# Attention and two feed-forward parts on one core: the identity for the row maxima read from PSUM instead of SBUF

## The chip, the cores and the metric

The kernel runs on one core of a Trainium2 chip. Its engines work beside one another and wait for each other through semaphores: TensorE (PE, with PEld for its weight loads), VectorE (DVE), ScalarE (ACT), GpSimd (POOL) and SyncE (SP), which issues most transfers. The metric is device time in microseconds (us), from several runs, and less is better.

## The reference, cut to what matters

First comes attention over 4 batches of 8 heads, with 576 positions of 64 features, in float32. It is causal by blocks of 64 positions. After it come two feed-forward parts, which the change doesn't touch.

```python
scores = scale * np.matmul(q, k.transpose(0, 1, 3, 2))
mask = block_i >= block_j                      # blocks of 64 positions
scores = np.where(mask, scores, -1000000000.0)
scores = scores - np.max(scores, axis=-1, keepdims=True)
attn = np.exp(scores)
attn = attn / (np.sum(attn, axis=-1, keepdims=True) + 1e-09)
return np.matmul(attn, v).astype(np.float32)
...
x = _moe_ref(x=x, **moe_kwargs)                # first feed-forward part
return _moe2_ref(x=x, **moe2_kwargs)           # second one, with a normalisation
```

## The kernel before, in words

The attention is a loop over 34 units: 32 heads ("h"), and two units ("z") for the first 64 positions of the batches, which are handled apart. A head's scores lie transposed in a PSUM tile `s` of 128 partitions by 1536 columns (three banks): partitions are keys, columns are queries. The list `SEG` says which key tile has which columns. Key tile 4 has only 64 keys, so in its 64 columns (960 to 1023 of the tile) only partitions 0 to 63 are of use; before the change its product is formed on all 128 partitions, with zeros for the missing keys.

A head goes through these steps, and each step of the loop holds one step of several heads.

- `em_A` forms the first products into `s` (five matrix products). It is sent a step ahead.
- `chain` finds the largest score of each query. VectorE reduces the five column ranges with a transposing maximum (L374), fills three places of `part` that belong to masked blocks with three memsets (L377), reduces again (L380), ScalarE brings four groups of 32 partitions together (`r<-r`, three instructions), VectorE reduces once more (L406) and writes the row of maxima on the diagonals of 32x32 blocks: the product of the maxima, broadcast, and a 32x32 identity, broadcast (L408). The result goes into 32 partitions of the right operand of the next products, `QK`.
- `em_B` adds the second products into `s` (five matrix products). They hold the low parts of queries and keys, the mask and, through the rows that L408 wrote, minus the maximum. So they wait for L408. Then ScalarE takes the exponential (`e<-s`).
- `em_PV` multiplies with the values (`p<-e,V`), and `norm` divides by the sums: VectorE by L455, L456 and L457, GpSimd by L458.

TensorE gets its work in the order em_A of head i+1, em_B of head i, em_PV of head i-1. The order on every engine is written out by hand. GpSimd meanwhile subtracts rounded parts from raw ones for later heads (L43, by `split_q` and `split_k`), and VectorE, ScalarE and GpSimd convert the weights of the first feed-forward part in between (L121, L125 on VectorE), at places that the table `PIECES` gives. The identity `eye` is a 128x128 tile in SBUF that a transfer brings at the start. `s` comes from a pool of two buffers, anew for each unit.

```python
tt(out=v3(dst)[:, x:x + 16],                     # L408
   in0=m[:, x:x + 16].unsqueeze(2).to_broadcast([32, 16, 32]),
   in1=eye[0:32, 0:32].unsqueeze(1).to_broadcast([32, 16, 32]), op=ALU.mult)
```

Of the kernel before, what the change touches and what calls it, by code (L numbers as in the profile page):

```python
# [25 lines left out]
GORD = (0, 3, 4, 2, 1)  # L26
# a head's score columns: (key tile, first query, queries, column)
SEG = [(0, 64, 512, 0), (1, 128, 448, 512), (4, 512, 64, 960), (2, 256, 320, 1024), (3, 384, 192, 1344)]
# [3 lines left out]
def attention_moe_kernel(ctx, tc, raw_d, dup_d, raw0_d, dup0_d, v_d, v0_d, msk_d, mz_d, vec_d, eye_d, wk_d, wv_d, wr_d, wc1_d, wc2_d, out_d):  # L32
# [43 lines left out]

    # A weight comes as the bits of a float64: sign, 11 bits of exponent, 52 of fraction. It
    # is loaded three bytes off, so that word 0 of its pair holds the exponent's low 4 bits
    # and 28 of the fraction, and byte 4 the sign and the exponent's high 7 bits, e. A
    # float32's sign and high 4 bits of exponent are those of e - 56, nothing below 56.  # L80
    CE = float(56 * 2 ** 27)

    def load_split(src, dst):
        """512 columns of a weight: as a float32, its rounded part and the rest; in steps, of one or two instructions."""
        st = {}
# [52 lines left out]
    def pieces(w, dst, k, n):  # L138
        """Rows 128k.. of w, n columns."""
        return [load_split(w[:, f:f + 512], lambda i, f=f: dst(i)[:, k, f:f + 512]) for f in range(0, n, 512)]  # L140

    class Convert:
        """Weight pieces on their way, one step per call."""

# [29 lines left out]

# [1 line left out]
    sp = opened(es_a, "as", 2, side=R)  # L176
# [16 lines left out]
    units.insert(IZ + 1, ("z", (1, 2, 3)))  # L193
    # The first 64 positions of several batches make one unit, whose operands lie where the
    # last weights come in later.
    wv0, wv1, wk0 = [w.rearrange("p k n -> p (k n)") for w in (*wv, wk[0])]
# [3 lines left out]
    LZ, QZ = wv1[:, 0:1536], wv1[:, 1536:3072]  # L200
    VZ = XT[B - 2][:, :, 65:577].rearrange("p b (k d) -> p b k d", d=128)
    N = len(units)
    idx = {u: i for i, u in enumerate(units)}
# [9 lines left out]
    def kz(a):  # L213
        """Batch a's operands of the first products, and its raw ones."""
        return KZ[:, 1024 * a - 1024:1024 * a], XT[B - 1][:, a - 1, 65:577]
# [17 lines left out]
    def make(u, who):  # L233
        """The first units' operands out of what load_raw brings, in parts, each by one of the engines."""
        t, n = u
        kl, qb = ops_B(u)
        raw = T.pop(("raw", u))
        w = 576 if t == "h" else 512
        if t == "z":
            kq = wk0[:, 0:1024]  # L240
        else:
            if n == 0:
                T["kq", 0] = lp.tile([128, 2, 1088], F32R, name="kq")
            kq = T["kq", 0][:, n]
        T["kq", u] = kq
        L, H, Q = slice(0, w), slice(w, w + 512), slice(w - 512, w)
        lo, up = slice(0, 64), slice(64, 128)

        def copy(x, out, in_):
            if x == "a":  # L250
                act(out, in_)
            else:
                (nc.vector if x == "d" else nc.gpsimd).tensor_copy(out=out, in_=in_)

        def less(x, out, in0, in1):
            sub(nc.vector if x == "d" else nc.gpsimd, out, in0, in1)

        return [
            lambda: copy(who[0], kq[lo, L], raw[lo, L]),
            lambda: copy(who[1], kq[up, H], raw[up, Q]),  # L260
            lambda: copy(who[2], kq[up, L], raw[lo, L]),
            lambda: copy(who[3], kq[lo, H], raw[up, Q]),
            lambda: less(who[4], kq[up, H], raw[up, Q], kq[up, H]),
            lambda: copy(who[5], qb[lo, Q], raw[up, Q]),
            lambda: less(who[6], kl[lo, L], raw[lo, L], kq[lo, L]),
        ]

    def joint_z(a, steps):
        """Batch a's part of what the joint unit needs."""
        kq, raw = kz(a)  # L270
# [24 lines left out]
    def tail_z(u):  # L295
        """Division by the sums, an instruction each."""
        n = len(u[1])
# [38 lines left out]
    def mm(out, lhsT, rhs, start, stop=True, **kw):  # L336
        nc.tensor.matmul(out=out, lhsT=lhsT, rhs=rhs, start=start, stop=stop, **kw)  # L337

    def em_A(u):
        s = ps.tile([128, 1536], F32, name="s")  # L340
        T["s", u] = s
        if u[0] == "h":
            kq = T["kq", u]
            for (j, q0, w, o) in SEG:
                mm(s[:, o:o + w], kq[:, 128 * j:128 * j + 128], kq[:, 512 + q0:512 + q0 + w], o % 512 == 0, skip_group_check=True)
        else:
            for x, b in enumerate(u[1]):
                kq = T["kq", u] if b == 0 else kz(b)[0]
                for o in range(0, 512, 128):
                    mm(s[:, 512 * x + o:512 * x + o + 128], kq[:, o:o + 128], kq[:, 512 + o:640 + o], o == 0, skip_group_check=True)  # L350

    def ops_B(u):
        """The second products' operands."""
        return (LZ, QZ) if u[0] == "z" else (KL[idx[u] % NB], QB[idx[u] % NB])

    def v3(ap):
        return ap.rearrange("p (b i) -> p b i", i=32)

    def chain(u):
        """From the first products to the row of maxima, in parts."""  # L360
        s = T["s", u]
# [4 lines left out]
        if u[0] == "h":  # L366
# [3 lines left out]
            def first():  # L370
                for (j, q0, w, o) in sorted(SEG, key=lambda x: x[0] == 0):
                    kp = 128 if j < 4 else 64
                    b0 = (q0 - 64) // 32
                    red(out=pt[0:kp, b0:b0 + w // 32, j], in_=v3(s[0:kp, o:o + w]), axis=AX.X, op=ALU.max, apply_transpose=True)  # L374
                for j in (1, 2, 3):
                    b0 = (128 * j - 64) // 32
                    ms(pt[64:128, b0:b0 + 2, j], -3.0e38)  # L377

# [13 lines left out]
        def mid():  # L392
# [14 lines left out]
        ] + [  # L407
            lambda x=x: tt(out=v3(dst)[:, x:x + 16], in0=m[:, x:x + 16].unsqueeze(2).to_broadcast([32, 16, 32]), in1=eye[0:32, 0:32].unsqueeze(1).to_broadcast([32, 16, 32]), op=ALU.mult)  # L408
            for x in range(0, nb, 16)
        ]  # L410

    def em_B(u):
# [4 lines left out]
        if u[0] == "h":  # L417
            for (j, q0, w, o) in SEG:
                mm(s[:, o:o + w], kl[:, 128 * j:128 * j + 128], qb[:, q0:q0 + w], False, skip_group_check=True)
            act(e, s, AF.Exp, scale=0.125)  # L420
        else:
            w = 512 * len(u[1])
            for o in range(0, w, 128):
                mm(s[:, o:o + 128], kl[:, o:o + 128], qb[:, o:o + 128], False, skip_group_check=True)
            act(e[:, 0:w], s[:, 0:w], AF.Exp, scale=0.125)

    def em_PV(u, x=0):
# [13 lines left out]
    def norm(u):  # L441
        """Division by the sums; parts for the step after em_PV(u)."""
        n = u[1]
# [16 lines left out]

# [1 line left out]
    def segs(g):  # L462
# [7 lines left out]
    def prep(g, kk, c, X):  # L470
        """A mixture of 128 features (by column c + kk of vec), split into X; in steps."""
        m = tmp.tile([128, GT], F32, name="mix")
# [71 lines left out]

# [1 line left out]
    groups = [(512 * i, min(512, NTOK - 512 * i)) for i in range(-(-NTOK // 512))]  # L546
# [74 lines left out]

    # When the first weights' steps come, by the attention's iterations: from the first one
    # on, a letter each. l: load; 1, 2: the exponent's two parts; x, y: the bits' two
    # instructions, X, Y: the same late in the iteration, B: x and Y; h: rounded; w, v, V: the
    # rest, by GpSimd or VectorE.
    PIECES = [
        (1, "l.12Bhw"), (4, "l12B.hw"), (6, "l12x.y.hw"), (9, "l1.2XyhV"), (17, "l12Bhv"),
        (21, "l12Bhw"), (22, "l12.x.yhw"), (27, "l12Bhw"), (29, "l12BhV"),
    ]
    # The joint unit's: its masks; per batch the load, three instructions and two engines;  # L630
    # its tail's ten instructions. Halves are late in an iteration.
    MASKS_Z = 2
    READY_Z = (4, 5.5, 10.5, 8.5, nc.gpsimd, nc.vector), (6, 11.5, 9.5, 13, nc.vector, nc.vector), (7, 12, 12.5, 12, nc.gpsimd, nc.gpsimd)
    TAIL_Z = 18, 18, 18.5, 20, 23, 22.5, 21, 23.9, 22.9, 21.9
    with tc.manual_schedule():
        # ---- attention, one step per unit
        plan = {}
# [11 lines left out]
        ms(eps, 1e-6)  # L649
        act(rsd[:, 0:1], eps, AF.Exp)  # loads the function's table  # L650
        ms(ce, -CE)
        for i in (0, 1):
            ms(part[i], -3.0e38)
        masks_z(0, 1)
        masks(1)
# [112 lines left out]

        # ---- the first feed-forward part
        es_h, es_r = ExitStack(), ExitStack()  # L770
# [55 lines left out]

        # ---- the second feed-forward part; its start runs beside the end of the first's
        es_f = ctx.enter_context(ExitStack())
# [50 lines left out]

        # the next weights' steps at three places of a step, by the group  # L880
        first = (0, 0, 0), (0, 0, 1), (0, 0, 0), (0, 1, 1), (1, 1, 2)
# [3 lines left out]
        def norms(x):  # L885
            """The next groups' part of the normalisation."""
            if x + 1 < len(GORD):
# [94 lines left out]
```

## Time and profile before

| what | value |
|---|---|
| median of 3 runs | 889.67 us |
| lowest and highest run | 888.71 and 891.22 us |
| span of the profiled execution, first to last instruction | 889.8 us |
| busy in the span: PE, DVE, ACT, POOL | 836.4, 558.3, 403.3, 266.8 us |
| mean granted TensorE clock | 0.983 of full speed |

The profile is of one execution. No other time of that execution is given than its span, which is 0.1 us above the median of the runs, so the span is used as its time. The attention takes about the first 220 us of it, the rest is the two feed-forward parts.

### The profile page before, as it was taken

How to read it: one execution, taken by the hardware profiler on the slowest of the kernel's cores; microseconds unless marked ns; L12 is line 12 of the kernel's file. 1: busy time of each engine (PE TensorE's matmuls, PEld its weight loads, DVE VectorE, ACT ScalarE, POOL GpSimd, SP SyncE). 2: the span in 40 equal slices, each digit the busy share in tenths (PEclk: the TensorE clock that was granted, in tenths of full speed). 3: DMA queues.
4: the chain of work that ended last, by engine and by line, in shares of the span. 5: the costliest groups of instructions: out<-in, count | busy, mean ns of one | idle time of the engine just before them, and what ended most of it. 6: DMA issues, size and time to landing. Idle time of an engine off the chain costs nothing. (4 is left out here: it accounts for less than half of the span.)

```text
span 889.8 us, 10495 instructions
## 1 busy us (share of the span) xinstructions
PE 836.4 (94%) x3824; PEld 678.8 (76%) x3824; DVE 558.3 (63%) x977; ACT 403.3 (45%) x689; POOL 266.8 (30%) x217
## 2 busy tenths in 40 slices
PE   4878888798978999999999999999999999999998
PEld 3555564565856898898898888888888888888886
DVE  6899899989899524414438756546555554536433
ACT  5867686778766543543554343312232222313110
POOL 6768567765577301101102311101101010101100
PEclk9989898989999999999999999999999999999999
DMA  9994366552332012001234311201111110201023
GB/s 241 286 311 154 123 207 217 161 161 63 121 127 72 12 60 71 23 14 36 72 142 127 122 40 56 72 24 48 47 49 48 48 48 24 71 1 48 1 95 118
DMA packets 40068, 83.65 MB, mean 94 GB/s; under 512 B 3472, under 2 KB 17936, under 8 KB 40016
## 3 DMA queue, kind: packets, MB, share of 16 engines
q1 hardware_dynamic: 34544, 60.61, 20.8%
q0 software_dynamic: 5040, 20.01, 7.5%
q10 hardware_dynamic: 432, 2.36, 0.8%
q8 instruction: 30, 0.49, 0.2%
q14 instruction: 22, 0.18, 0.1%
HBM read 71.17 MB, written 11.80 MB: 93 GB/s over the span
## 5 line engine op out<-in xcount | busy, mean ns | idle before, releaser
L337 PE MATMUL ph<-xn,c 128*128 128x512 f32 (+1 forms) x960 | 205.6, 369 | 0.0
L337 PE MATMUL po<-c,h 128*128 128x512 f32 x864 | 204.3, 391 | 0.4 <-DVE acc L618 0.4
L337 PEld LDWEIGHTS ph<-xn,c 128*128 128x128 f32 x960 | 167.9, 188 | 31.8
L337 PEld LDWEIGHTS po<-c,h 128*128 128x128 f32 x864 | 161.5, 188 | 35.6 <-DVE acc L618 1.2
L40 ACT ACTIVATE h<-ph 128x512 fp32r<-128x512 f32 (+1 forms) x80 | 42.9, 553 | 220.1 <-PE ph L337 220.1
L43 POOL TENSOR_TENSOR c<-a,c 128x512 fp32r<-128x512 f32 x32 | 42.1, 1317 | 310.3 <-ACT c L40 240.0
L604 DVE SCALAR_TENSOR_TENSOR h<-ph,h 128x512 fp32r<-128x512 f32 (+1 forms) x80 | 49.8, 636 | 129.5 <-ACT h L40 129.5
L618 DVE TENSOR_TENSOR acc<-po,acc 128x512 f32<-128x512 f32 x144 | 97.8, 688 | 45.7 <-PE po L337 43.8
L337 PE MATMUL p<-e,V 128*128 128x512 f32 (+4 forms) x320 | 112.6, 483 | 0.0
L337 PE MATMUL s<-x,wk 128*128 128x384 f32 x576 | 103.5, 339 | 1.3 <-DVE x L43 1.2
L337 PEld LDWEIGHTS s<-x,wk 128*128 128x128 f32 x576 | 101.3, 188 | 3.2 <-DVE x L43 1.4
L40 ACT ACTIVATE a<-raw,ce 128x512 f32<-128x512 int8 x93 | 66.9, 754 | 77.1 <-DVE a L125 58.5
L337 PE MATMUL p<-wv,k 128*128 128x512 f32 x432 | 99.4, 390 | 0.0
L337 PEld LDWEIGHTS p<-e,V 128*128 128x128 f32 (+1 forms) x320 | 56.7, 202 | 49.6 <-issue 42.4
L337 PEld LDWEIGHTS p<-wv,k 128*128 128x128 f32 x432 | 80.9, 188 | 16.5
L43 POOL TENSOR_TENSOR x<-mix,x 128x384 fp32r<-128x384 f32 x36 | 41.6, 1172 | 156.2 <-ACT x L40 152.9
L43 DVE TENSOR_TENSOR k<-a,k 128x768 fp32r<-128x768 f32 x24 | 23.6, 983 | 81.6 <-ACT a L40 81.5
L374 DVE TRANSPOSE_TENSOR_REDUCE part<-s 128x14 f32<-128x448 f32 (+4 forms) x160 | 64.5, 460 | 5.5 <-PE s L337 4.9
L125 DVE SCALAR_TENSOR_TENSOR a<-raw,a 128x512 int32<-128x512 int32 x52 | 58.8, 1130 | 3.8
L40 ACT ACTIVATE e<-s 128x1536 f32<-128x1536 f32 (+1 forms) x34 | 48.3, 1421 | 28.4 <-PE s L337 28.2
L337 PE MATMUL s<-QK 128*128 128x512 f32 (+4 forms) x160 | 35.2, 353 | 26.7 <-DVE QK L408 25.9
L337 PE MATMUL s<-wr,x 128*128 128x512 f32 x216 | 53.4, 407 | 6.3 <-ACT x L40 5.3
(105 smaller groups left out, 894.3 us busy)
## 6 DMA issues: line engine op xcount, KB each, us to landing
kq<-in_dup_dram POOLq DMA_DIRECT2D x15, 1088.0 KB, 5.7
raw<-in_raw_dram SPq DMA_DIRECT2D x32, 288.0 KB, 4.9
raw<-in_w_ch_dram SPq DMA_DIRECT2D x16, 511.6 KB, 3.7
raw<-in_w_ch_dram SPq DMA_DIRECT2D x32, 255.6 KB, 3.1
V<-in_v_dram SPq DMA_DIRECT2D x16, 320.0 KB, 4.6
x_scr<-r SPq DMA_DIRECT2D x18, 256.0 KB, 2.0
acc<-x_scr SPq DMA_DIRECT2D x18, 256.0 KB, 4.7
out_dram<-acc SPq DMA_DIRECT2D x18, 256.0 KB, 2.0
```

The costliest lines, as they stand in the source:

```text
L40: nc.scalar.activation(out=out, in_=in_, func=func, **kw)
L43: eng.tensor_tensor(out=out, in0=in0, in1=in1.bitcast(F32), op=ALU.subtract)
L125: stt(out=st["a2"].bitcast(I32), in0=w3, scalar=5, in1=st["a1"].bitcast(I32), op0=ALU.logical_shift_right, op1=ALU.bitwise_or)
L337: nc.tensor.matmul(out=out, lhsT=lhsT, rhs=rhs, start=start, stop=stop, **kw)
L374: red(out=pt[0:kp, b0:b0 + w // 32, j], in_=v3(s[0:kp, o:o + w]), axis=AX.X, op=ALU.max, apply_transpose=True)
L604: stt(out=h1[1][:, m, 0:n], in0=p[:, 0:n], scalar=0.0, in1=h1[0][:, m, 0:n].bitcast(F32), op0=ALU.max, op1=ALU.subtract)
L618: tt(out=acc[i], in0=p, in1=acc[i], op=ALU.add)
```

## The change: what it does

The two tiles for scores are taken from the pool once (`SC`) and used in turn. In each, a 32x32 identity is kept in partitions 64 to 95 of columns 960 to 991, where no useful score lies. So that nothing overwrites it, the products of key tile 4 are cut to 64 columns of weights and write partitions 0 to 63 alone, in `em_A` and in `em_B` (`seg`). ScalarE writes the identity (`put_eye`) at the start, after VectorE has filled the place with zeros, and once more after the joint unit of three batches, which uses the whole tile. L408 of a head reads its second operand from there; L408 of the two "z" units reads `eye` as before. The three memsets at L377 become one whose pattern visits the same places. The other lines of the diff only drop comments.

```diff
+    SC = [ps.tile([128, 1536], F32, name="s") for _ in range(2)]
...
+    def seg(x, j):
+
+        k = 128 if j < 4 else 64
+        return x[:, 128 * j:128 * j + k], slice(0, k)
+
+    def put_eye(s):
+        act(s[64:96, 960:992], eye[64:96, 64:96])
+
     def em_A(u):
-        s = ps.tile([128, 1536], F32, name="s")
+        s = SC[idx[u] % 2]
...
             for (j, q0, w, o) in SEG:
-                mm(s[:, o:o + w], kq[:, 128 * j:128 * j + 128], kq[:, 512 + q0:512 + q0 + w], o % 512 == 0, skip_group_check=True)
+                k, P = seg(kq, j)
+                mm(s[P, o:o + w], k, kq[:, 512 + q0:512 + q0 + w], o % 512 == 0, skip_group_check=True)
...
+    def strided(x, *steps):
+
+        return bass.AP(x.tensor, x.offset, [list(x.ap[0])] + [list(a) for a in steps])
...
-                for j in (1, 2, 3):
-                    b0 = (128 * j - 64) // 32
-                    ms(pt[64:128, b0:b0 + 2, j], -3.0e38)
+
+                ms(strided(pt[64:128, 2:4, 1], [21, 3], [5, 2]), -3.0e38)
...
-            lambda x=x: tt(out=v3(dst)[:, x:x + 16], in0=m[:, x:x + 16].unsqueeze(2).to_broadcast([32, 16, 32]), in1=eye[0:32, 0:32].unsqueeze(1).to_broadcast([32, 16, 32]), op=ALU.mult)
+            lambda x=x: tt(out=v3(dst)[:, x:x + 16], in0=m[:, x:x + 16].unsqueeze(2).to_broadcast([32, 16, 32]), in1=(s[64:96, 960:992] if u[0] == "h" else eye[0:32, 0:32]).unsqueeze(1).to_broadcast([32, 16, 32]), op=ALU.mult)
...
             for (j, q0, w, o) in SEG:
-                mm(s[:, o:o + w], kl[:, 128 * j:128 * j + 128], qb[:, q0:q0 + w], False, skip_group_check=True)
+                k, P = seg(kl, j)
+                mm(s[P, o:o + w], k, qb[:, q0:q0 + w], False, skip_group_check=True)
             act(e, s, AF.Exp, scale=0.125)
...
             act(e[:, 0:w], s[:, 0:w], AF.Exp, scale=0.125)
+            if w > 960:
+                put_eye(s)
...
         for i in (0, 1):
             ms(part[i], -3.0e38)
+            ms(SC[i][64:128, 960:1024], 0.0)
+            put_eye(SC[i])
```

## Rows read from the trace of the kernel before

**Rows 1.** Stretch, length; busy PE, PEld, DVE, ACT, POOL; clock; DMA share, GB/s.

```profile
16.00:212.00 196.00, 166.30 (x664) 110.27 (x663) 176.43 (x430) 144.63 (x261) 135.85 (x106) 0.93 0.63 197
212.00:300.00 88.00, 79.66 (x345) 63.54 (x345) 74.76 (x88) 60.56 (x101) 55.34 (x45) 0.98 0.27 87
300.00:889.00 589.00, 585.33 (x2802) 500.72 (x2800) 297.46 (x433) 188.48 (x310) 66.43 (x51) 1.00 0.17 57
```

**Rows 2.** Waits between 16 and 212 us: total, times, longest.

```profile
PE s L337 <- DVE QK L408: 24.9, 19, 3.5
DVE m L406 <- ACT r L40: 8.6, 17, 1.6
```

**Rows 3.** Page, costliest groups: the first reductions; idle time before them at the end.

```profile
L374 DVE TRANSPOSE_TENSOR_REDUCE part<-s 128x14 f32<-128x448 f32 (+4 forms) x160 | 64.5, 460 | 5.5 <-PE s L337 4.9
```

**Rows 4.** Line L408, durations in ns: least, median, most.

```profile
L408 DVE TENSOR_TENSOR QK<-m,eye x32: 682/1078/1731, 16.2 to 211.8; 32x512 fp32r<-32x512 f32 x32
```

**Rows 5.** Groups of VectorE to 260 us: busy us, mean ns of one.

```profile
L408 DVE TENSOR_TENSOR QK<-m,eye 32x512 fp32r<-32x512 f32 x32 | 35.7, 1115 | 1.1
...
L121 DVE TENSOR_TENSOR a<-a,a 128x512 int32<-128x512 f32 x9 | 14.3, 1594 | 0.0
```

**Rows 6.** Timeline around two L408: start, duration, engine; idle time in brackets.

```profile
131.86 0.68 DVE L408 TENSOR_TENSOR QK<-m,eye 32x512 fp32r<-32x512 f32 x1
...
132.58 0.71 DVE L457 STREAM_TRANSPOSE RB<-r 128x512 f32<-128x512 f32 x1
...
133.21 1.99 DVE L374 TRANSPOSE_TENSOR_REDUCE part<-s 128x14 f32<-128x448 f32 x5
133.46 1.27 POOL L458 TENSOR_TENSOR XT<-U,RB 128x512 f32<-128x512 f32 x1 [2.88 <-ACT U L40]
...
162.26 1.62 POOL L43 TENSOR_TENSOR kq<-raw,kq 64x512 fp32r<-64x512 f32 x1
...
162.91 1.53 DVE L408 TENSOR_TENSOR QK<-m,eye 32x512 fp32r<-32x512 f32 x1
```

**Rows 7.** Timeline of POOL and DVE in the second feed-forward part.

```profile
540.00 1.32 POOL L43 TENSOR_TENSOR c<-a,c 128x512 fp32r<-128x512 f32 x1 [1.29 <-ACT c L40]
540.45 1.29 DVE L604 SCALAR_TENSOR_TENSOR h<-ph,h 128x512 fp32r<-128x512 f32 x2 [1.19 <-ACT h L40]
```

**Rows 8.** Line L604, durations in ns: least, median, most.

```profile
L604 DVE SCALAR_TENSOR_TENSOR h<-ph,h x80: 412/691/693, 486.4 to 875.5; 128x512 fp32r<-128x512 f32 x64, 128x256 fp32r<-128x256 f32 x16
```

**Rows 9.** Timeline of one head's three memsets and the next reduction.

```profile
130.24 0.08 DVE L377 MEMSET part<- 64x2 f32 x3
130.39 0.24 DVE L380 TENSOR_REDUCE r<-part 128x16 f32<-128x80 f32 x1
```

**Rows 10.** Timeline of TensorE over one em_PV and the next em_A.

```profile
159.65 3.22 PE L337 MATMUL p<-e,V 128*128 128x512 f32 x10
...
160.53 0.19 PEld L337 LDWEIGHTS p<-e,V 128*128 128x128 f32 x1 [0.24 <-issue]
...
161.37 1.20 PEld L337 LDWEIGHTS p<-e,V 64*128 64x128 f32 x6 [0.65 <-issue]
...
162.57 1.07 PE L337 MATMUL s<-kq 128*128 128x512 f32 x5
```

**Rows 11.** Start of the kernel: ACT in order of time, and one transfer.

```profile
2.03 0.20 ACT L40 ACTIVATE rsd<-eps 128x1 f32<-128x1 f32 x1
5.42 1.27 ACT L40 ACTIVATE wk<-raw 64x512 fp32r<-64x512 f32 x2 [3.19 <-DMA raw<-in_raw_dram]
7.13 1.32 ACT L40 ACTIVATE kq<-raw 64x576 fp32r<-64x576 f32 x2 [0.44 <-DMA raw<-in_raw_dram]
...
10.18 0.63 ACT L40 ACTIVATE kq<-raw 64x512 fp32r<-64x512 f32 x1 [1.21 <-DMA raw<-in_raw_dram]
...
1.65 0.42 SPq L647 DMA_DIRECT2D eye<-in_eye_dram  x1
...
eye<-in_eye_dram SPq DMA_DIRECT2D x1, 64.0 KB, 6.0
```

## Prediction, made before the changed kernel ran

> **What bounds the kernel now.** I read the busy times by stretch first, then the waits of the attention, then the single instructions of L408 and their neighbours in the timeline. After 300 us TensorE is busy 585.3 of 589 us, and the change touches nothing there; from 212 to 300 us it is busy 79.7 of 88. So what the attention gains or loses arrives at the end unchanged, and the place to look is the stretch from 16 to 212 us [rows 1]. There VectorE is the busiest engine, 176.4 of 196 us, while TensorE is busy 166.3 and idle 29.7 [rows 1]. Of that idle time 24.9 us, at 19 heads, ends with L408 [rows 2]. VectorE itself hardly waits: 8.6 us for the three small ScalarE copies before L406 [rows 2], and 4.9 us in the whole kernel for the first products before L374 [rows 3]. The rest of its idle time, some 6 us, is the few hundredths between instructions. The loop is thus paced by VectorE, and TensorE stands at L408.
>
> L408 always has the same shape, yet takes from 682 to 1731 ns, with a median of 1078 [rows 4]. The timeline shows why. At 131.86 us it takes 0.68 us; GpSimd is idle then, for the 2.88 us up to 133.46. At 162.91 us it takes 1.53 us: GpSimd's L43 runs from 162.26 to 163.88, and L408 ends 0.56 after that, so nearly all of its work is done once GpSimd is through [rows 6]. Both of its operands are in SBUF, as are L43's, and it stands still while GpSimd reads. An instruction of VectorE with one operand in PSUM and one in SBUF doesn't: two L604 together took 1.29 us from 540.45 on, the first of them wholly beside a GpSimd product from 540.00 to 541.32 [rows 7], and over all 80 of them none is above 693 ns [rows 8].
>
> **The change part by part.**
>
> *L408's operand.* Removed is the stretch beyond 0.682 us: 32 x (1.115 - 0.682) = 13.9 us of VectorE [rows 4, 5]. L604 says that PSUM costs next to nothing extra at 512 elements (0.691) [rows 8]. Bounds: 0, if the remaining SBUF operand still collides, and 13.9. Since VectorE paces the loop I take most of it, 11.0; the discount of a fifth is for the stretches in which TensorE is late on its own. [...]
>
> *Three memsets into one.* From the first memset to the next reduction are 0.15 us for three, of which the three together take 0.08 [rows 9]; one alone can't take less than its share of 0.03, so at best 0.05 goes, at worst nothing. I take 0.02 x 32 = 0.6 us gained.
>
> *The overlap behind L408.* L374 starts at 133.21, 0.08 us before L457 ends (132.58 + 0.71); L457 starts 0.04 after L408 has ended [rows 6]. No row shows if L374 may still overlap when the last PSUM operand before it began at partition 64. If not, a head loses 0.08 + 0.04 = 0.12 us, at most 3.8 for 32; where L374 follows L408 directly nothing changes. I take 1.0 lost. [...]
>
> *Products of key tile 4 on 64 columns.* They lie in the middle of each group of five. No row shows a 64-column weight tile. The nearest is em_PV, whose middle product has 64 rows: two passes of 512 columns take (160.53 - 159.65)/2 = 0.44 us each, so 3072 columns take 2.64 us, and em_PV took 162.57 - 159.65 = 2.92 [rows 10]. The remaining 0.28 us bounds from above what leaving and entering the whole array costs a group; the weight load there came after 0.65 us of idle time instead of 0.24, so it was not fetched ahead [rows 10]. From below it is nothing, as a load of half the columns is no longer than a whole one. I take 0.25, near the row: 64 groups, 16 us of TensorE. They are hidden in its idle time: 29.7 - 11 = 18.7 us are left [rows 1, 2]. That cover is thin, so I charge 2.0 for heads where it isn't there. If the cover were gone, all 16 would count. [...]
>
> *The start.* put_eye stands in ScalarE's queue before the copies of the first unit and waits for `eye`. That is issued at 1.65 and lands 6.0 later, at 7.65 [rows 11]; two small copies of some 0.2, as the smallest one there takes [rows 11], bring 8.1. The copies at 5.42 then start 2.7 later. Behind them ScalarE was idle 0.44 and 1.21 [rows 11], which absorb 1.65. So 1.0 arrives at the first maxima, and the bounds are 0 and 2.7. VectorE's two fills of PSUM lie before 5.4 us, when it waits anyway.
>
> *What moves.* The `s` tiles are no longer taken anew; em_A waits for the same exponential as before. No transfer and no queue of SP or POOL is moved. put_eye after the joint unit is one copy, two steps ahead of its reader. What may change by itself is how the conversions meet GpSimd: L121, with both operands in SBUF, takes 1.594 in the mean [rows 5], against 0.69 for an undisturbed instruction of this size [rows 8]: 9 x 0.90 = 8 us that can shrink or grow as GpSimd's work slides, and L125's likewise. GpSimd also stops waiting for L408. [...]
>
> Sum: -11.0 - 0.6 + 1.0 + 2.0 + 1.0 - 1.0 - 1.0 = -9.6 us on 889.8, which is **880.2**. The span is 0.1 above the median of the runs, so the same number stands for the median.
>
> **The rivals.**
>
> [...]
> - *TensorE becomes the bound:* with x per group, its stretch is 166.3 + 64 x, plus the 4.8 of its idle time that L408 doesn't end (29.7 - 24.9). At x = 0.28 that is 189.0 and still 7 faster; at x = 0.35 it is 193.5, 2.5 faster, less 1.0 at the start: 888.
> - *Slower, by the same place at a higher price:* from x = 0.39 on TensorE alone needs more than 196 us. If each of the two switches costs what I put for the pair, x = 0.56, 206.9 us, and the time is 889.8 + 10.9 + 1.0 = 902. Against it: em_PV has two switches inside its 0.28. [...]
> - *The change doesn't do what it says:* L408 goes on colliding through its operand `m` in SBUF. Then -0.6 + 1.0 + 1.0 + 1.0 for TensorE, some 892. Against it stand 80 L604, none above 693 ns [rows 8].
>
> **How the numbers follow.** My forecast, 875 to 886, 0.62; more than that, 870 to 875, 0.10; TensorE the bound, 884 to 891, 0.13; slower through the switches, 0.07; no relief, 891 to 893, 0.08. Within 0.3% (2.7 us, about what a measurement of this kernel can tell from no change) lie half of the third and half of the last. Faster by more: 0.62 + 0.10 + 0.06 = 0.78; same 0.11; slower 0.11. The range 872 to 889 leaves out the two last cases, a part of the third and the lower end of the second, some 0.2. The likeliest case's own range is 875 to 886.
>
> **What would show it.** L408 of the heads at 0.68 to 0.70 us throughout; the wait of TensorE for L408 down from 24.9 to under 12; VectorE's busy time in the attention down by some 14 us or more; after the 64-column product a gap of about 0.25 us in each group; em_A of the first unit some 2 us later than before. The prediction is wrong if TensorE's idle time in the attention falls to almost nothing while the time stays, if L408 still spreads, or if the start costs several us.

## The result, and the profile after

The changed kernel takes 875.41 us (median of 4 runs, 875.01 to 876.41). The kernel before, run beside it, takes 889.94 us (4 runs, 888.71 to 891.22). The ratio is 0.9833, with a 95% interval of 0.9817 to 0.9849: 14.5 us less. The forecast was 880.2, so the direction and the place were right and the gain was 5 us larger than put.

One correction first. The profiled execution of after has a span of 873.5 us and a run time of 875.24, so some 1.7 us lie outside the span. The prediction took the span of before, 889.8, for a run time. Its own time is not on record; most likely it was the run of 891.22, the first of its list, as the profiled one is the first in every other list. If so, the two profiled executions differ by 16.3 us in the span and 16.0 in time, while the medians differ by 14.5; the terms below are counted in the spans.

The first lines of the profile's page of after, its span and the busy time of each engine:

```profile
span 873.5 us, 10455 instructions
...
PE 831.3 (95%) x3824; PEld 675.1 (77%) x3824; DVE 543.8 (62%) x915; ACT 403.5 (46%) x692; POOL 261.8 (30%) x217
```

Now the stretches of after, with the columns of [rows 1]. The last L408 (L423 in the new numbering) starts at 195.2 instead of 211.8, so 16 to 196 is the stretch that answers to 16 to 212 of before:

```profile
16.00:196.00 180.00, 160.51 (x667) 104.78 (x666) 162.12 (x369) 145.83 (x266) 131.62 (x107) 0.97 0.68 215
...
212.00:300.00 88.00, 81.42 (x355) 68.17 (x354) 69.12 (x83) 51.08 (x85) 50.13 (x42) 0.94 0.26 87
300.00:873.00 573.00, 569.00 (x2729) 487.20 (x2728) 287.93 (x416) 182.57 (x296) 63.37 (x48) 1.00 0.17 58
```

VectorE is busy 162.1 of 180 us, 90%, as it was with 176.4 of 196 [rows 1]. The loop is shorter and still paced by the same engine. TensorE is idle 19.5 us in it instead of 29.7. In the feed-forward parts nothing has changed: 4.0 us of idle TensorE after 300 us, 3.7 before [rows 1].

Line L423 of after by its durations, as [rows 4] (least, median, most, in ns), the heads first:

```profile
L423 DVE TENSOR_TENSOR QK<-m,s x32: 685/685/686, 17.0 to 195.2; 32x512 fp32r<-32x512 f32 x32
L423 DVE TENSOR_TENSOR wv<-mz,eye x3: 1486/1749/1882, 91.7 to 95.0; 32x512 fp32r<-32x512 f32 x3
```

All 32 heads take 685 ns, where they spread from 682 to 1731 [rows 4]. The joint unit's three instructions, which still read `eye` in SBUF, go on spreading. The two traces show what stretched them. Before, 19 of the 32 took more than 700 ns. At each of these a GpSimd instruction was running when L408 started, and L408 ended 0.545 to 0.556 us after that instruction did. At the other 13, of 682 to 684 ns, no GpSimd instruction was running. After, 20 of the 32 ran beside a GpSimd instruction, and all took 685 or 686 ns. One of these, to be set beside the 1.53 us of [rows 6]:

```profile
152.45 1.61 POOL L43 TENSOR_TENSOR kq<-raw,kq 64x512 fp32r<-64x512 f32 x1
...
153.09 0.69 DVE L423 TENSOR_TENSOR QK<-m,s 32x512 fp32r<-32x512 f32 x1
```

From the first head's L408 to the last one's are 178.2 us, where it was 195.6 [rows 4]: 17.4 less.

The waits of after up to 240 us (total, times, longest), as [rows 2]:

```profile
PE s L340 <- DVE QK L423: 14.7, 17, 2.6
...
DVE m L421 <- ACT r L40: 9.1, 18, 1.7
```

TensorE's wait for L408 falls from 24.9 us [rows 2] to 14.7. It does not vanish: VectorE still paces the loop, and TensorE still waits at 17 heads.

VectorE's groups of before up to 260 us, those that were not shown among [rows 5] (busy us, mean ns of one, then idle time in front):

```profile
L374 DVE TRANSPOSE_TENSOR_REDUCE part<-s 128x14 f32<-128x448 f32 x32 | 20.2, 632 | 5.5 <-PE s L337 4.9
...
L377 DVE MEMSET part<- 64x2 f32 x96 | 2.5, 60 | 1.9
```

And the same view of after (L390 is L374, L392 is L377):

```profile
L423 DVE TENSOR_TENSOR QK<-m,s 32x512 fp32r<-32x512 f32 x32 | 21.9, 685 | 1.1
L390 DVE TRANSPOSE_TENSOR_REDUCE part<-s 128x14 f32<-128x448 f32 x32 | 20.9, 652 | 4.1 <-PE s L340 3.3
...
L121 DVE TENSOR_TENSOR a<-a,a 128x512 int32<-128x512 f32 x9 | 15.5, 1727 | 0.0
...
L392 DVE MEMSET part<- 64x6 f32 x32 | 2.0, 63 | 2.0
```

L408 has lost 35.7 - 21.9 = 13.8 us, which is the 13.9 of [rows 4, 5] that stretching cost. The memsets went from 2.5 to 2.0.

VectorE's conversions L125 in the loop, from 16 to 212 us of before and from 16 to 196 us of after:

```profile
L125 DVE SCALAR_TENSOR_TENSOR a<-raw,a 128x512 int32<-128x512 int32 x8 | 10.3, 1293 | 0.2
```

```profile
L125 DVE SCALAR_TENSOR_TENSOR a<-raw,a 128x512 int32<-128x512 int32 x9 | 8.1, 902 | 0.2
```

Counted between the first and the last L408 of a head, with overlaps given to the earlier instruction, VectorE's time changed so: L408 -13.8, L125 -2.9, its L43 -1.0, memsets -0.5, L374 +2.1, L121 +1.2; busy time -15.0 in all (-14.9 by these), idle time -2.5, of it -1.6 in the wait of the first reduction for TensorE (4.9 to 3.3 in the fences above). That is the loop's -17.4. The smaller terms scatter: in a second execution of the same changed kernel, traced later, L125 took 0.8 us less and the idle time was 0.7 us longer.

### The profile page after: what moved, and what is told of

The parts are those of the page before. It is cut to its first block, busy times and chain, and to the rows that moved or that the text cites. A ratio compares the mean times of both kernels' runs of the same rounds, so it can differ in the third digit from the quotient of the medians.

```text
span 873.5 us, 10455 instructions
## 1 busy us (share of the span) xinstructions
PE 831.3 (95%) x3824; PEld 675.1 (77%) x3824; DVE 543.8 (62%) x915; ACT 403.5 (46%) x692; POOL 261.8 (30%) x217
## 5 line engine op out<-in xcount | busy, mean ns | idle before, releaser
L43 POOL TENSOR_TENSOR c<-a,c 128x512 fp32r<-128x512 f32 x32 | 42.1, 1318 | 310.1 <-ACT c L40 239.7
L340 PE MATMUL p<-e,V 128*128 128x512 f32 (+4 forms) x320 | 106.4, 462 | 0.0
L340 PEld LDWEIGHTS p<-e,V 128*128 128x128 f32 (+1 forms) x320 | 54.5, 194 | 45.4 <-issue 38.3
L43 POOL TENSOR_TENSOR x<-mix,x 128x384 fp32r<-128x384 f32 x36 | 41.6, 1171 | 156.8 <-ACT x L40 153.5
L43 DVE TENSOR_TENSOR k<-a,k 128x768 fp32r<-128x768 f32 x24 | 23.6, 982 | 82.0 <-ACT a L40 81.9
L390 DVE TRANSPOSE_TENSOR_REDUCE part<-s 128x14 f32<-128x448 f32 (+4 forms) x160 | 65.1, 465 | 4.1 <-PE s L340 3.3
L125 DVE SCALAR_TENSOR_TENSOR a<-raw,a 128x512 int32<-128x512 int32 x52 | 55.8, 1074 | 3.9
L340 PEld LDWEIGHTS s<-wr,x 128*128 128x128 f32 x216 | 42.4, 198 | 15.4 <-ACT x L40 4.5
```

The lines of the kernel that those rows point to most:

```text
L43: eng.tensor_tensor(out=out, in0=in0, in1=in1.bitcast(F32), op=ALU.subtract)
L125: stt(out=st["a2"].bitcast(I32), in0=w3, scalar=5, in1=st["a1"].bitcast(I32), op0=ALU.logical_shift_right, op1=ALU.bitwise_or)
```

## The experiments

Three explanations were open. *The operand:* L408 alone carries the gain, because it no longer has two operands in SBUF. *The rest of the change:* narrow products, fixed tiles and one memset carry part of it, or cost something that the operand's gain hides. *The place:* only the identity in PSUM helps, and not the maxima there.

**The identity back in SBUF, all else as changed.**

```diff
-in1=(s[64:96, 960:992] if u[0] == "h" else eye[0:32, 0:32])
+in1=eye[0:32, 0:32]
```

> The changed kernel with one thing undone: L408 of a head reads the identity from SBUF again; the 64-column products, the fixed score tiles, the copies of the identity and the one memset stay. Theory (the gain is that L408 no longer has two operands in SBUF and so no longer stands still beside GpSimd): the time goes back to that of the kernel before, 888 to 891 us, L408 of the heads spreads from 0.68 to about 1.7 us again with a sum of some 35 us, and TensorE's wait for it is 22 to 28 us. Rival (the narrower products or the tiles that are no longer taken anew carry it): 875 to 881 us, with L408 spread all the same.

It took 890.61 us against 889.76 of before, ratio 1.0013 (0.9998 to 1.0027). Line L423 of this kernel, durations, and TensorE's wait for it up to 240 us:

```profile
L423 DVE TENSOR_TENSOR QK<-m,eye x32: 682/888/1732, 16.9 to 210.7; 32x512 fp32r<-32x512 f32 x32
```

```profile
PE s L340 <- DVE QK L423: 23.1, 18, 3.5
```

The spread is back, and so is the time. Narrow products, fixed tiles, the copies of the identity and the single memset together cost between -0.2 and +2.4 us, by the interval. Within that, all of the gain hangs on the operand.

**The operand in PSUM for the odd heads only, then for the even heads only.** The collisions are not evenly spread. [rows 6] show why: at 131.86 L408 is followed by L457, for whose result GpSimd is waiting just then (2.88 us idle up to 133.46). The row's bracket names ScalarE's `U`; but L458 starts 0.17 us after L457 has ended, as it does at 14 of its 16 places. GpSimd is waiting like this at most of the even-numbered heads. At 15 of the 16 odd ones a GpSimd instruction is running when L408 starts, at only four of the even ones. Of the 13.9 us, 11.8 lie at the odd heads.

```diff
-(s[64:96, 960:992] if u[0] == "h" else eye[0:32, 0:32])
+(s[64:96, 960:992] if u[0] == "h" and u[1] % 2 else eye[0:32, 0:32])
```

> The changed kernel, but only the odd heads read the identity from PSUM; the even ones read SBUF. In the trace before, the excess of L408 over 0.682 us is 11.8 us at the 16 odd heads and 2.1 at the even ones, since GpSimd waits for VectorE's division just when an even head's L408 comes. Theory (collision with GpSimd): nearly all of the gain stays, 876 to 879 us. Rival (an operand in PSUM is worth the same at each head, or the rest of the change carries the gain): half of it, 881 to 884, or all of it in both halves.

873.22 us (4 runs, 870.41 to 876.67), ratio 0.9835 (0.9803 to 0.9867; the quotient of the medians alone would be 0.9814). All of the gain stays, and the median lies 2.8 us under the range that was put. L423 of this kernel:

```profile
L423 DVE TENSOR_TENSOR QK<-m,eye x16: 682/683/1409, 16.9 to 185.4; 32x512 fp32r<-32x512 f32 x16
L423 DVE TENSOR_TENSOR QK<-m,s x16: 685/685/686, 22.4 to 190.4; 32x512 fp32r<-32x512 f32 x16
```

The other half, with `u[1] % 2 == 0` as the condition:

> The other half: only the even heads read the identity from PSUM. Theory: little of the gain stays, 885 to 890 us, and the odd heads' L408 stay at 1.2 to 1.7 us. Rival (the same worth at each head): 881 to 884 us.

889.58 us, ratio 0.9998 (0.9982 to 1.0014):

```profile
L423 DVE TENSOR_TENSOR QK<-m,s x16: 685/685/685, 18.2 to 204.5; 32x512 fp32r<-32x512 f32 x16
L423 DVE TENSOR_TENSOR QK<-m,eye x16: 682/1492/1733, 23.3 to 209.5; 32x512 fp32r<-32x512 f32 x16
```

So 16 of the 32 operands carry all of the gain that can be told from nothing. The even heads that stay in SBUF have a median of 683 ns; the odd ones that stay there, 1492, as the order of GpSimd's work says. The same instruction, with the same operands, is stretched or not by what GpSimd does beside it. In the five other kernels here that have such an L408, 41 took more than 700 ns, and each ended 0.54 to 0.56 us after a GpSimd instruction that was running when it started, as the 19 of before did.

**The three memsets back, all else as changed.**

> The changed kernel with the three memsets at each head. Theory: they cost the loop 0.02 us a head, so 0.4 to 0.7 us slower than the changed kernel, 875.5 to 876.5 us. Rival (each VectorE instruction costs a start of its own, 0.06 us): 32 x 0.12 = 3.8 us slower, 879 us.

877.29 us (875.51 to 878.75), ratio 0.9867 (0.9846 to 0.9888). The median is 0.8 us above the range that was put and 1.9 above that of after, but the intervals touch (0.9849 and 0.9846). The loop from the first to the last L408 is 178.2 us in both, which speaks against the rival's 3.8 us, and the first L408 stands 1.4 us later here, for a reason that wasn't looked for. In the trace the memsets are worth half a microsecond; in the time they can't be told from nothing.

**The other operand: the maxima in PSUM, the identity in SBUF.** Before, with one line edited; wide products, a tile per unit and three memsets stay. L406 writes its 16 maxima into the unused place of `s`:

```diff
-m = cz.tile([32, nb], F32, name="mz") if nb > 16 else sp.tile([32, 16], F32, name="m")
+m = cz.tile([32, nb], F32, name="mz") if nb > 16 else s[64:96, 960:976] if u[0] == "h" else sp.tile([32, 16], F32, name="m")
```

> The kernel before with one edit: the row of maxima m of a head (32 partitions by 16) is written by L406 into the unused partitions 64 to 95, columns 960 to 975, of the score tile, and L408 reads it there; the identity stays in SBUF. So the other operand of L408 is in PSUM, and there are no narrower products, no fixed tiles, no identity in PSUM, no copy at the start, and three memsets. Theory (either operand in PSUM ends the collision): L408 at 0.68 to 0.70 us at all heads, and 874 to 877 us: the gain of 14.5 us, plus 0.7 for the start that isn't held up, less 0.5 for the memsets. Rival (it must be the identity, or the narrower products or the fixed tiles matter): L408 still spreads, 886 to 891 us.

876.65 us against 889.11, ratio 0.9867 (0.9845 to 0.9888). L408 and TensorE's wait for it in this kernel:

```profile
L408 DVE TENSOR_TENSOR QK<-s,eye x32: 689/689/690, 16.7 to 196.4; 32x512 fp32r<-32x512 f32 x32
```

```profile
PE s L337 <- DVE QK L408: 14.5, 18, 2.7
```

Either operand in PSUM ends the stretching. The one line gives 12.5 of the 14.5 us without any of the rest. With the single memset as well:

```diff
+ms(strided(pt[64:128, 2:4, 1], [21, 3], [5, 2]), -3.0e38)
```

> The kernel before with the maxima in PSUM, as the run before the last, and the three memsets as one. Expected 0.4 to 0.7 us under that run, some 873.5 to 876 us, and under the changed kernel by the start, 0.5 to 1 us. If the narrower products or the fixed tiles had a worth of their own, it would be slower than the changed kernel.

875.16 us, ratio 0.984 (0.9817 to 0.9862). That is 1.5 us under the run before it and 0.3 under the changed kernel, where 0.4 to 0.7 and 0.5 to 1 were put; the intervals overlap. It is the same as the whole change, with products of 128 columns, which is a second sign that the narrow ones neither cost nor give.

**The identity written later at the start.** The two copies stand behind the first unit's in ScalarE's queue instead of ahead of them.

> The changed kernel with the two copies of the identity moved on ScalarE behind the copies of the first two units, so that nothing of the first unit waits for the identity's transfer. Theory (the start costs 0.7 us, as the first head's L408 came at 16.97 instead of 16.23 us): 874 to 875.2 us, and the first L408 at about 16.2 us. Rival (the delay is taken up by later waits): no change, 875 to 876 us.

875.40 us, ratio 0.985 (0.9827 to 0.9873): no gain. ScalarE at the start of after, in order of time, then of this kernel:

```profile
7.46 0.31 ACT L40 ACTIVATE s<-eye 32x32 f32<-32x32 f32 x2 [5.23 <-DMA eye<-in_eye_dram]
7.80 1.27 ACT L40 ACTIVATE wk<-raw 64x512 fp32r<-64x512 f32 x2
...
11.61 0.67 ACT L40 ACTIVATE r<-r 32x8 f32<-32x8 f32 x3
```

```profile
5.31 1.27 ACT L40 ACTIVATE wk<-raw 64x512 fp32r<-64x512 f32 x2 [3.08 <-DMA raw<-in_raw_dram]
...
10.78 0.63 ACT L40 ACTIVATE kq<-raw 64x512 fp32r<-64x512 f32 x1 [1.74 <-DMA raw<-in_raw_dram]
11.43 0.67 ACT L40 ACTIVATE r<-r 32x8 f32<-32x8 f32 x3
```

The first copies come 2.5 us earlier and the first maxima 0.2: a later copy waits for its transfer, here 1.74 us. The first L408 comes at 16.8 us instead of 17.0, not at the 16.2 that was put. So the wait for the identity is hidden but for at most 0.2 us, and a second execution of the changed kernel differs by as much (its first L408 comes at 17.2). The 0.7 by which after starts later than before is within what the start differs by from kernel to kernel: the first L408 of a head stands at 16.2 us before [rows 4] and at 16.4 to 18.3 in the kernels tried here. The theory that the copies cost 0.7 falls.

**Is there a better one?** The odd heads alone had come out 2.2 us under the whole change. It was run again, beside the whole change, and beside the one-line version with the maxima in PSUM for the odd heads only.

> The kernel before with one memset a head and with the maxima in PSUM for the odd heads alone; the even heads keep both operands in SBUF. Theory of the hold (an L408 that reads PSUM from partition 64 on keeps the next L374 from overlapping with the instruction before it, 0.1 us a head; at the even heads there is little collision to win, so they do better without): 872 to 875 us, at or under the changed kernel and the run with all heads' maxima in PSUM. Rival (the difference between all heads and odd heads alone was scatter): 875 to 876.5 us.

> The changed kernel as it is, on the same chip and in the same call as the two versions with odd heads alone: 874.5 to 876.5 us.

> The changed kernel with the identity read from PSUM by the odd heads alone, again, to tell if it is faster than the changed kernel. Theory of the hold: 1.5 to 2.5 us under the changed kernel of this call, 873 to 874 us. Rival (scatter): within 1 us of it.

The maxima of odd heads: 873.98 us (871.0 to 879.21), ratio 0.9834 (0.9806 to 0.9862). The whole change: 875.81, 0.985 (0.983 to 0.987). The identity for odd heads: 875.75, 0.9855 (0.9834 to 0.9875). The repeat lies within 0.1 us of the whole change, so the lead was scatter, as the rival said. The maxima of odd heads lie in the range of the theory, but their runs spread over 8 us and all three intervals overlap: none is shown to beat the change. The last of the three still answers a question of its own. VectorE around an even head of it, whose L423 reads SBUF alone:

```profile
157.81 0.68 DVE L423 TENSOR_TENSOR QK<-m,eye 32x512 fp32r<-32x512 f32 x1
158.52 0.71 DVE L475 STREAM_TRANSPOSE RB<-r 128x512 f32<-128x512 f32 x1
159.16 1.99 DVE L390 TRANSPOSE_TENSOR_REDUCE part<-s 128x14 f32<-128x448 f32 x5
```

L390 starts 0.07 before L475 ends (158.52 + 0.71), as in [rows 6]. In the first run of the whole change it starts after that end, around the same head:

```profile
158.32 0.69 DVE L423 TENSOR_TENSOR QK<-m,s 32x512 fp32r<-32x512 f32 x1
159.03 0.71 DVE L475 STREAM_TRANSPOSE RB<-r 128x512 f32<-128x512 f32 x1
159.06 1.05 PE L340 MATMUL s<-QK 128*128 128x512 f32 x5 [0.34 <-DVE QK L423]
159.78 2.04 DVE L390 TRANSPOSE_TENSOR_REDUCE part<-s 128x14 f32<-128x448 f32 x5
```

Against the whole change run beside it, the first reductions take 1.3 us less in this kernel's loop, and the L408 take 1.7 us more, since the even heads' collide again: the two nearly cancel.

## Why the prediction was right, and where its sum was off

**What bounds the loop: right.** VectorE paces it, TensorE stood at L408, and what the attention gained arrived at the end: the loop lost 17.4 us and the span 16.3.

**L408's operand: the mechanism right, the size too small.** It is shown from both sides: the identity in SBUF brings the 682 to 1732 ns back, either operand in PSUM ends them, and the odd heads, where GpSimd is at work, carry all of it. Each stretched L408 ended some 0.55 us after the GpSimd instruction that it had met. The step from L604 [rows 7, 8] held to 6 ns (685 for 691), and with either operand in PSUM L408 takes 685 to 690 ns. The term was put at -11.0 and measured -13.8. The discount of a fifth, for stretches in which TensorE is late on its own, was not needed: the first reduction's wait for TensorE fell, 4.9 to 3.3 us, where it should have grown.

**Products on 64 columns: the step that failed.** They were put at +2.0, with 0.25 us for a group, by the nearest row, em_PV's product of 64 rows [rows 10]. They cost nothing that can be seen. In the median a group of five takes 1.070 us in em_A, 1.069 before, and 1.046 in em_B, 1.045 before. Inside em_A's groups, from the 448-column product to the 64-column one and on to the 320-column one, starts lie 0.200 and 0.029 us apart in the median, 0.201 and 0.028 before. Weight loads of after, mean ns of one after the comma:

```profile
L340 PEld LDWEIGHTS s<-kq 128*64 128x64 f32 x32 | 4.5, 139 | 1.5
...
L340 PEld LDWEIGHTS s<-QK 128*128 128x128 f32 x128 | 20.0, 197 | 22.5 <-DVE QK L423 18.0 <-issue 1.2 <-POOL QK L43 0.6
```

A load of 64 columns takes 139 ns, and 197 for 128, and the next load follows as before. em_PV's 64-row load keeps its gap, here in after:

```profile
160.83 0.19 PEld L340 LDWEIGHTS p<-e,V 128*128 128x128 f32 x1 [0.24 <-issue]
161.67 1.20 PEld L340 LDWEIGHTS p<-e,V 64*128 64x128 f32 x6 [0.65 <-issue]
162.84 0.90 PEld L340 LDWEIGHTS s<-kq 128*128 128x128 f32 x5
```

The group of em_A behind it, which took 1.07 us before [rows 10]:

```profile
162.87 1.08 PE L340 MATMUL s<-kq 128*128 128x512 f32 x5
```

So a tile of 64 columns did not cost what one of 64 rows does, and the row chosen for the bound was the wrong kind. The two differ in more than that: em_PV sends ten products for its five key tiles, em_A five. What makes the gap of the 64-row one wasn't tried. With the term fall both rivals in which TensorE pays for switches; x is 0.

**The overlap behind L408: the mechanism right, the term too small.** +1.0 was put, with 3.8 as the upper bound; it is +2.7. Before, L374 started 0.076 us ahead of the end of its predecessor at 19 of 31 heads, behind 10 of 12 L457, all five L125 and four others; after, it starts 0.01 to 0.03 us behind that end at all of these. At these 19, L374 ends 2.66 us later in all against its predecessor's end: 2.02 for the later starts (19 x 0.106), 0.65 because it takes 0.03 longer in the mean without the overlap, which the prediction's 0.12 a head had left out. In the account above 2.1 of it stand with L374 and 0.6 in the idle time. Where it follows L408 directly, the 0.031 was there before and stays, as put. The even heads of the last experiment, whose L408 reads no PSUM, overlap again: L390 starts ahead of L475's end at ten of them. The 3.8 was too much, since only 19 heads had an overlap to lose.

**Memsets:** 0.6 put, 0.5 measured in the trace, not to be seen in the time.

**The start:** +1.0 put, 0.7 seen; the late copies show that the wait for the identity makes at most 0.2 of it. em_A of the first unit did come 2.0 us later (its weights at 9.1 instead of 7.2), and the idle times behind absorbed most of it, by the mechanism put. With the late copies the first maxima still came 0.6 us later than before, behind a transfer; so that the term came near its number was in part luck.

**What moves by itself:** -1.0 each was put for the conversions and for the clock, the last two terms of the sum. Of the conversions, L125 gave -2.9, L43 on VectorE -1.0, and L121 took +1.2: -2.7. L125's gain was not designed: before, its three longest started 0.50 us into a GpSimd instruction and took 1.79 us; after, four of the eight started some 1.4 us into one and took 0.80. GpSimd did stop waiting for L408: before, nine of its L43 on `kq` and `QK` started while a head's L408 ran, and took 1.62 us (`kq`, two) and 1.74 to 1.75 (`QK`, seven); after, four did, and took 1.28 to 1.29 (`kq`, three) and 1.41 (`QK`, one). VectorE's idle time fell by 2.5, where 1.0 was put for the clock; that term no run shows. TensorE's time at a granted clock of 0.50 fell from 27 to 10 us in the loop (0.93 and 0.97 in the mean), and its idle time from 29.7 to 19.5; VectorE, which paces the loop, waited 1.6 us less for TensorE, so little of the gain can be the clock's; how much was not separated. From 212 to 300 us the time at 0.50 grew from 3 to 10 us (0.98 and 0.94 in the mean), though TensorE's idle time fell there too, from 8.3 to 6.6. Of the loop's 17.4 less the start's 0.7, the stretch behind gave back 0.4; whether by the clock wasn't separated.

Summed again with what was measured: -13.8 - 0.5 + 2.1 + 0 + 0.7 - 2.7 - 2.5 = -16.7, and the span fell by 16.3. Put was -9.6. Of the difference of 7.1, 2.8 are L408's discount, 2.0 the switches, 1.7 the conversions and 1.5 the idle time; the other terms nearly cancel (-0.9 of gain). The medians differ by 1.8 less than the spans, most of it because before's profiled execution was probably the slowest of its runs.

**Of the signs named:** L408 at 0.68 to 0.70 and em_A's 2 us were seen. VectorE's busy time fell by 14.3 us, from 176.4 [rows 1] to 162.1. The wait of TensorE for L408 was to fall under 12 and is 14.7, and the gap after the 64-column product is absent.

## What to carry to other kernels

When one instruction of VectorE has a spread of durations at a constant shape, look what GpSimd does beside its long and its short ones, and count its operands in SBUF: here one small operand moved to PSUM, by a single line, was worth 1.3%. Before pricing such an edit, list every cost by the row of the same kind: a narrower weight tile was priced by a shorter one and the price was wrong altogether. And an overlap of 0.08 us between two instructions can hang on what a third one read before them; here it took back 2.7 us of the gain.

## What the runs showed of the hardware that was not expected

- A weight tile of 64 columns between tiles of 128 cost TensorE nothing (groups of 1.07 us in em_A and 1.05 in em_B, in the median, as before), while the load of one of 64 rows in em_PV came 0.65 us behind the one before, where full ones have 0.24.
- The collisions of VectorE and GpSimd sat almost wholly in every second head (11.8 of 13.9 us), since at most of the others GpSimd stood waiting for VectorE.
- L121, with SBUF operands alone, went on colliding when L408 no longer did: 1.594 to 1.727 us in the mean. Nine of them take 15.5 us. Each of those over 700 ns ended 0.54 to 0.56 us after a GpSimd instruction beside it, as L408 did. Giving L121 an operand in PSUM wasn't tried.
